# A planner that lets parts of a TensorE block finish on their own, a floor folded into a factor, and a new table of moved turns

## The chip, the cores and the metric

The kernel runs on one core of a Trainium2 chip. The metric is the device time of one execution in microseconds (us); three executions of the kernel before took 788.7, 790.91 and 790.98 us, median 790.91. Engines are named as the profile names them: PE (TensorE; PEld are its weight loads), DVE (VectorE), ACT (ScalarE), POOL (GpSimd) and SP (SyncE, which here only issues DMAs).

## What is computed

Block-sparse attention over 4 batches, 8 heads, 768 positions and head size 64, followed by a feed-forward layer over the 3072 tokens:

```python
scores = scale * np.matmul(q, k.transpose(0, 1, 3, 2))
scores = np.where(mask, scores, -1000000000.0)
attn = np.exp(scores - np.max(scores, axis=-1, keepdims=True))
attn = attn / (np.sum(attn, axis=-1, keepdims=True) + 1e-09)
x = np.matmul(attn, v)            # (4, 8, 768, 64) -> (3072, 512)
h = x @ w_in                      # (512, 2048)
out = np.maximum(0.01 * h, h) @ w_out
```

A query block of 32 positions sees its neighbours, the first and the last block, and three drawn blocks; the first and the last query block see all keys. The weights come in as 64-bit floats and are decoded on the chip.

## The kernel before

**The work.** Every wide product is made of 16-bit halves: an operand is scaled by a power of two, rounded to a high half, and the rest is kept as a low half, so that a product is two or three 16-bit matmuls. The scale comes from a *sum*: ACT squares the tile and adds along the row, `scale_sum` (L699) adds over the 128 rows by a 32-bit matmul with a matrix of ones into a corner of a PSUM bank, and `scale_of` (L706) takes half the exponent on DVE, multiplies by 2^50 and takes the reciprocal. So that a sum of nothing gives no infinity, `scale_sum` first multiplies the ones with a tiny constant tile, `floor` (L696), into the same place. There are 52 such sums: 24 for halves of q, 16 for k, 8 for the weights, 4 for v.

**The units.** Queries go in 12 tiles T of 64 positions for each batch, four tiles make an *item* (12 items), and in a tile the 8 heads make 4 units, two of which make a pair. A unit is: two score products on PE (`s`, keys and queries in both halves, in quarters of the array), mask, scale and minimum on DVE (`p`, `mx`), exponent on ACT (`p`, `sum`), normalising, splitting in halves on ACT and DVE (`pp`), transposing (`pt`: by PE in the first 16 units, later by a DMA that SP issues), and the product with gathered values on PE (`av`, in halves of the array). After the last pair of a tile, ACT, DVE, ACT and POOL make the halves of `x` from `av` (`avt`, `xf`, `x`). When an item's four tiles are done, its feed-forward layer can run: blocks of 12 matmuls `h<-x,W`, then `ht` (ACT, DVE), `g` (DVE or ACT, POOL), then blocks of 6 matmuls `o<-W,g`. Items 0 and 1 run it quarter by quarter, as the weights become ready.

**The weights.** Each quarter of `w_in` and `w_out` is loaded, decoded on ACT and DVE, summed (`sq` products and a sum on PE, `ssw`) and split. For four of the eight quarters the low half is made on PE: `h<-W,dg` (32-bit, 128x512), `h<-W,eye`, into one bank that ACT has to empty (`W<-h`) before the next such block may write it. There are 16 of these *low-half blocks*.

**What sets the order.** The function records all work as tasks (class `Task`, L149; `Plan.task` and `Plan.add`). A PE `block()` joins several matmuls into one task, up to the scores of two units and the `av` of an earlier pair. `Plan.trial` (L328) then plays the tasks on a model of the engines, with costs written down in `COST`, and takes the ready task with the smallest number on each engine; the order that comes out is issued as it is, and each engine runs its own queue in that order. Before a PE task may start in the model, a margin is added when what released it was a DMA (`margin`, 900 ns) or when it is a sum (`margin_sum`, 1500 ns). `SHIFTS` (L168) is a table of (engine, time, length, amount): `Plan.order` (L484) adds the amount to the numbers of the tasks that a first trial started in that time, and runs the trial again. In the kernel before, a joined task releases everything that depends on it when all of it has ended, and its mode of the array is that of its last member:

```python
g.busy += busy + (COST["change"].get((g.kind, kind), 0) if g.run[1:] else 0)
g.late = late
g.kind = kind
```

Of the kernel before, what the change touches and what calls it, by code (L numbers as in the profile page):

```python
# [27 lines left out]
TINY = 2.0 ** -60  # L28
# [120 lines left out]
class Task:  # L149
    __slots__ = ("eng", "run", "busy", "late", "reads", "writes", "prio", "kind", "loads", "need", "then", "n", "gate",  # L150
                 "port")
# [5 lines left out]
    "margin": 900.0,  # L157
    "margin_sum": 1500.0,
# [10 lines left out]
    ("SP", 4453, 107, -1500), ("ACT", 155, 28, 250), ("ACT", 1623, 42, 250), ("all", 2175, 27, 250),  # L169
    ("ACT", 1595, 75, -250), ("PE", 3567, 8, 250), ("all", 6881, 11, -60), ("POOL", 2481, 37, -1500),  # L170
    ("DVE", 2721, 75, -250), ("PE", 6073, 3, -900), ("all", 4828, 11, 500), ("DVE", 3064, 28, 500),
    ("all", 5445, 45, 500), ("all", 3572, 11, 500), ("PE", 6937, 2, 500), ("all", 5557, 144, -500),
    ("SP", 2109, 9, 1500), ("all", 3954, 10, -120), ("PE", 7061, 46, 900), ("PE", 4358, 7, 500),
    ("SP", 1544, 125, 250), ("DVE", 3641, 14, -500), ("PE", 3570, 156, 120), ("DVE", 439, 83, 250),
    ("all", 1197, 83, 60), ("all", 3834, 40, -1500), ("PE", 2617, 26, -500), ("all", 4058, 9, -500),
    ("DVE", 4951, 4, -1500), ("all", 7040, 6, 1500), ("SP", 1817, 33, -250), ("all", 1599, 39, 120),
    ("ACT", 2034, 160, -500), ("all", 3979, 53, -500), ("ACT", 823, 3, 1500), ("PE", 2781, 20, -1500),
    ("DVE", 1339, 35, 1500), ("PE", 4476, 23, -500), ("PE", 4234, 54, -30), ("PE", 6696, 16, -500),
    ("all", 6350, 25, -60), ("DVE", 3344, 34, -900), ("ACT", 654, 7, 500), ("SP", 4785, 91, -500),
    ("DVE", 857, 84, 500), ("POOL", 3003, 70, 250), ("all", 3974, 83, 30), ("PE", 3328, 4, -250),  # L180
    ("DVE", 4105, 2, -1500), ("all", 1984, 11, -1500), ("PE", 3910, 108, 30), ("ACT", 4072, 54, 500),
    ("PE", 1273, 116, 900), ("PE", 1646, 2, -1500), ("PE", 5096, 36, 120), ("all", 7064, 64, 900),
    ("DVE", 1867, 192, 1500), ("POOL", 669, 93, -900), ("SP", 5579, 138, 900), ("ACT", 711, 129, -500),
    ("PE", 4092, 28, -30), ("PE", 2891, 45, 900), ("ACT", 1809, 27, -1500), ("PE", 2615, 16, 500),
    ("PE", 242, 38, 1500), ("all", 5757, 48, 250), ("DVE", 681, 191, 120), ("all", 1863, 25, -250),
    ("PE", 3995, 27, 500), ("SP", 739, 12, -500), ("DVE", 2593, 12, -1500), ("POOL", 143, 58, -1500),
    ("all", 4808, 128, -250), ("all", 5582, 105, 900), ("all", 7636, 41, 250), ("ACT", 2745, 174, 250),
# [3 lines left out]
    ("DVE", 6056, 7, -1500), ("DVE", 2679, 12, -500), ("POOL", 683, 26, 1500), ("all", 5932, 143, 120),  # L191
    ("PE", 5689, 13, 500), ("all", 6366, 5, 250), ("DVE", 1298, 4, 60), ("ACT", 2130, 10, 1500),
    ("DVE", 5753, 47, -900), ("PE", 4075, 46, -60), ("all", 5372, 4, -250), ("PE", 5734, 101, -120),
    ("all", 3970, 3, 120), ("PE", 6430, 172, -250), ("all", 131, 68, 900), ("all", 65, 92, 120),
    ("ACT", 4121, 11, -250), ("PE", 5573, 139, -120), ("PE", 2951, 76, -1500), ("DVE", 5810, 37, 900),
    ("all", 6716, 21, -1500), ("SP", 1552, 11, -1500), ("SP", 136, 8, -500), ("all", 4371, 54, 30),
    ("all", 4733, 84, -120), ("all", 4547, 19, -250), ("PE", 4602, 93, 60), ("all", 1807, 15, -60),
    ("PE", 4207, 100, 120), ("PE", 5966, 6, 250), ("DVE", 5925, 3, 500), ("all", 6695, 132, -60),
    ("DVE", 4349, 101, -1500), ("all", 4763, 97, 60), ("ACT", 2129, 13, 500), ("ACT", 4420, 147, -60),
    ("all", 4756, 16, 250), ("all", 3010, 5, 1500), ("all", 5803, 120, 30), ("all", 2525, 13, -900),  # L200
    ("PE", 2438, 62, -60), ("SP", 2869, 195, 1500), ("POOL", 4611, 7, 1500), ("POOL", 2710, 114, 500),
    ("PE", 4304, 5, 250), ("DVE", 2744, 140, -900), ("PE", 5737, 55, 60), ("DVE", 376, 5, -500),
    ("POOL", 3144, 20, 900), ("all", 5714, 4, 500), ("PE", 7203, 8, 1500), ("all", 134, 126, 1500),
    ("DVE", 2375, 119, -1500), ("DVE", 2552, 6, 900), ("DVE", 2551, 8, -1500), ("PE", 5631, 87, 250),
    ("SP", 2697, 169, 500), ("ACT", 2503, 45, -1500), ("all", 1624, 29, -250), ("SP", 1855, 73, 900),
    ("POOL", 724, 24, -60), ("DVE", 3566, 39, 60), ("DVE", 2426, 132, -900), ("SP", 2127, 28, 500),
# [3 lines left out]
    ("all", 2131, 13, -500), ("DVE", 5346, 193, 250), ("all", 1563, 83, -250), ("ACT", 1620, 84, -30),  # L210
    ("all", 2583, 13, 250), ("DVE", 4829, 140, 900), ("PE", 2578, 30, -250), ("DVE", 735, 14, -900),
    ("all", 767, 51, -250), ("all", 5404, 5, 1500), ("all", 0, 121, -1500), ("PE", 3062, 14, 500),
    ("all", 758, 37, -250), ("all", 5575, 15, -1500), ("DVE", 778, 4, 500), ("all", 3842, 25, 900),
    ("all", 3298, 16, 900), ("all", 1710, 3, -1500), ("DVE", 2941, 124, 500), ("DVE", 2096, 9, 1500),
    ("DVE", 898, 54, 1500), ("SP", 106, 7, 900), ("SP", 5620, 11, 900), ("all", 4754, 152, 60),
    ("PE", 4115, 68, -900), ("PE", 5237, 5, -500), ("all", 2823, 6, 1500), ("all", 7288, 42, 120),
    ("all", 105, 8, -1500), ("all", 3761, 45, -30), ("PE", 5743, 31, 250), ("ACT", 2345, 6, 1500),
    ("all", 4021, 87, 500), ("all", 4084, 29, -500), ("ACT", 1983, 162, -900), ("ACT", 3007, 29, 1500),
    ("PE", 4982, 46, -500), ("all", 129, 44, -250), ("PE", 4110, 92, -500), ("all", 5578, 7, 1500),
    ("SP", 79, 4, 1500), ("all", 3562, 12, 250), ("all", 2681, 4, 500), ("PE", 3379, 195, -60), ("POOL", 837, 5, 60),  # L220
    ("DVE", 4095, 107, -30), ("all", 2632, 7, 250), ("SP", 749, 13, 900), ("SP", 4851, 192, 900),
    ("PE", 4409, 15, -250), ("DVE", 2501, 150, 250), ("PE", 3618, 10, -900), ("DVE", 4553, 8, -1500),
    ("PE", 5456, 27, -250), ("all", 4402, 3, 250), ("all", 180, 9, -500), ("POOL", 718, 6, 900), ("PE", 5497, 9, 500),
    ("PE", 3378, 27, 500), ("all", 835, 6, -250), ("ACT", 4560, 49, -900), ("ACT", 5706, 92, 1500),
    ("DVE", 4151, 81, 120), ("all", 0, 101, -900), ("all", 57, 4, 30), ("PE", 5545, 31, 250), ("PE", 5488, 185, -30),
    ("POOL", 3172, 124, -500), ("DVE", 5716, 40, -500), ("all", 3342, 17, -30),
# [27 lines left out]
class Plan:  # L254
# [10 lines left out]
    def task(self, eng, run, busy, late, reads, writes, kind="", loads=(), port=False):  # L265
        if self.group is not None and eng == self.group.eng:
            g = self.group
            g.run.append(run)
            g.busy += busy + (COST["change"].get((g.kind, kind), 0) if g.run[1:] else 0)
            g.late = late  # L270
            g.reads |= reads
            g.writes |= writes
            g.kind = kind
            g.loads += loads
            return
        t = Task()
        t.eng, t.run, t.busy, t.late, t.kind, t.loads, t.port = eng, [run], busy, late, kind, list(loads), port
        t.reads, t.writes = reads, writes
        self.add(t)

    def add(self, t):
        t.prio, t.n, t.then, t.gate = self.prio, len(self.tasks), [], self.gate
        self.prio += 1.0
        need = set()
        for c in t.reads:
            need.update(self.wrote.get(c, ()))
# [41 lines left out]
    def trial(self, prio, stay):  # L328
# [102 lines left out]
        while events:  # L431
# [24 lines left out]
            elif what == "landed":  # L456
# [3 lines left out]
                if not need[i]:  # L460
                    finish(t, i)
# [1444 lines left out]
```

## Time and profile before

| | us |
|---|---|
| median of three executions | 790.91 |
| lowest and highest | 788.7, 790.98 |
| the profiled execution | 783.51 |
| its span, first to last instruction | 781.5 |
| PE busy | 724.3 (93%) |
| DVE busy | 546.0 (70%) |
| ACT busy | 471.0 (60%) |
| POOL busy | 364.1 (47%) |

The page gives one profiled execution. A row of a group or of the timeline names the engine, the operation, `out<-in` by the program's tile names, the shape, the count, and for a group the busy time and the mean of one; in square brackets stands how long the engine had been idle before, and who ended that. PE's ends are modelled; its starts are not. All work recorded by the planner stands under one line, L531 in the kernel before and L502 in the changed one, so groups are told apart by their tiles.

### The profile page before, as it was taken

Reading aid. Unit: us, or ns where it says so; the run is one execution under the profiler, and the core shown is the slowest. Engines: PE = TensorE matmul, PEld = TensorE weight load, DVE = VectorE, ACT = ScalarE, POOL = GpSimd, SP = SyncE. Lnnn points to the kernel's source line nnn. Section 1 sums busy time; section 2 is a strip of 40 time slices with the busy share of each in tenths; the row PEclk is TensorE's granted clock in tenths of the full one; section 3 lists DMA queues with packets and bytes.
Section 4 is the critical chain, followed back from the end, with each engine's and each line's share of the span. In section 5 each row is a group of like instructions: output and inputs, shape, how many; then the busy total and the mean of one; then the engine's idle time right before and its main releaser. Section 6 shows DMA issues by size and latency. Waiting matters only on the chain. (4 is left out here: it accounts for less than half of the span.)

```text
span 781.5 us, 21520 instructions
## 1 busy us (share of the span) xinstructions
PE 724.3 (93%) x8036; PEld 486.8 (62%) x8036; DVE 546.0 (70%) x1545; ACT 471.0 (60%) x1111; POOL 364.1 (47%) x626
## 2 busy tenths in 40 slices
PE   5575799898999999999999999999999999999997
PEld 5353545466566666666666757666766767666664
DVE  4888679798966787679666677778766766763131
ACT  7789578785874667667466566666565555452111
POOL 4407343444735375566434465555335655442131
PEclk9677599999999999999999999999999999999999
DMA  9629768996879699997996898979675764644100
GB/s 198 246 79 274 215 203 174 231 200 139 195 165 208 97 190 190 217 190 148 200 189 129 135 198 170 205 139 205 147 150 99 147 158 89 136 99 60 34 1 28
DMA packets 261940, 122.64 MB, mean 157 GB/s; under 512 B 230220, under 2 KB 242636, under 8 KB 261836
## 3 DMA queue, kind: packets, MB, share of 16 engines
q1 hardware_dynamic: 254796, 98.20, 62.4%
q0 software_dynamic: 7040, 23.07, 11.7%
q8 instruction: 63, 1.03, 0.6%
q14 instruction: 41, 0.34, 0.2%
HBM read 65.65 MB, written 12.58 MB: 100 GB/s over the span
## 5 line engine op out<-in xcount | busy, mean ns | idle before, releaser
L531 PE MATMUL h<-x,W 128*128 128x256 f16 x2304 | 271.7, 274 | 6.8 <-ACT x L531 3.0
L531 PEld LDWEIGHTS <-W 128*128 128x128 f16 (+1 forms) x2480 | 239.0, 100 | 58.2 <-issue 17.4
L531 PE MATMUL o<-W,g 128*128 128x512 f16 x1152 | 265.6, 379 | 0.3 <-DVE W L531 0.2
L531 POOL TENSOR_TENSOR g<-ht,g 128x512 f16<-128x512 f32 x96 | 116.2, 1211 | 221.8 <-DVE g L531 116.5
L531 PEld LDWEIGHTS <-g 128*128 128x128 f16 x1152 | 109.6, 98 | 122.5 <-issue 6.8
L531 DVE SCALAR_TENSOR_TENSOR pp<-p,r,pp 128x256 f16<-128x256 f32 (+1 forms) x208 | 123.2, 622 | 24.9 <-ACT pp L531 24.4
L531 ACT ACTIVATE p<-p,mx 128x256 f32<-128x256 f32 (+1 forms) x208 | 107.2, 517 | 39.8 <-DVE mx L531 39.1
L1258 POOL DMA_INDIRECT vg<-scr,vrow x88 | 91.1, 1036 | 75.9 <-PE av L531 60.5
L531 ACT ACTIVATE ht<-h,gs 128x512 f32<-128x512 f32 x80 | 54.8, 685 | 116.3 <-PE h L531 73.7
L531 DVE SCALAR_TENSOR_TENSOR ht<-h,gd,ht 128x512 f32<-128x512 f32 x80 | 59.9, 749 | 92.4 <-ACT ht L531 91.9
L531 ACT ACTIVATE pp<-p,r 128x256 f16<-128x256 f32 (+1 forms) x208 | 98.2, 515 | 36.6 <-issue 14.3
L1225 POOL COPY kg<-kt 128x128 int32 x264 | 82.2, 348 | 63.3 <-PE s L531 60.7
L531 DVE CUSTOM_DVE_ANT_0 p<-s,em,nsc 128x256 f32<-128x256 f32 x176 | 80.5, 477 | 12.9 <-PE s L531 12.2
L531 PE MATMUL av<-pt,vg 128*64 128x64 f16 (+1 forms) x2112 | 54.9, 208 | 3.3 <-ACT pp L531 1.9
L531 PEld LDWEIGHTS <-vg 128*64 128x64 f16 x2112 | 46.0, 114 | 14.5 <-issue 13.6
L531 PE MATMUL s<-kg,qs 128*32 128x256 f16 x704 | 47.2, 281 | 7.7 <-DVE r L531 3.0
L531 PEld LDWEIGHTS <-qs 128*32 128x32 f16 (+1 forms) x768 | 25.5, 96 | 38.7 <-issue 31.7
L531 DVE COPY kg<-kt 128x512 f16<-128x512 f16 x96 | 46.4, 506 | 0.8 <-PE s L531 0.8
L531 PE MATMUL s<-kg,qxs 128*32 128x256 f16 x704 | 46.4, 276 | 0.4 <-DMA qxs<-qs 0.4
L531 DVE CAST g<-ht 128x512 f16<-128x512 f32 x80 | 35.4, 443 | 14.5 <-PE o L531 11.4
L531 POOL TENSOR_TENSOR x<-xf,x 128x256 f16<-128x256 f32 x48 | 36.2, 755 | 20.0 <-ACT x L531 19.6
L531 ACT ACTIVATION_READ_ACCUMULATOR p<-p,mx 128x1 f32 x208 | 39.4, 189 | 0.0
(132 smaller groups left out, 783.7 us busy)
## 6 DMA issues: line engine op xcount, KB each, us to landing
v<-in_v_dram SPq DMA_DIRECT2D x32, 192.0 KB
qxs<-qs SPq DMA_DIRECT2D x48, 128.0 KB
scr<-v SPq DMA_DIRECT2D x16, 384.0 KB
vg<-scr SPq DMA_DIRECT2D x44, 128.0 KB
rq<-in_q_dram SPq DMA_DIRECT2D x20, 256.0 KB
W<-in_moe_w_in_dram SPq DMA_DIRECT2D x5, 1024.0 KB
out_dram<-ob SPq DMA_DIRECT2D x20, 256.0 KB
rk<-in_k_dram SPq DMA_DIRECT2D x24, 192.0 KB
```

The costliest lines, as they stand in the source:

```text
L531: self.plan.task(self.eng, lambda: f(*a, **k), busy, late, reads, writes, kind, loads, port)
L1225: tc.nc.gpsimd.tensor_copy(out=kg.ap.bitcast(I32)[:, :, slot * BLOCK // 2:(slot + 1) * BLOCK // 2], in_=kt.ap.bitcast(I32)[:, :, bass.ds(o ...
L1258: tc.nc.gpsimd.indirect_dma_start(into.ap, None, scr[b].ap, bass.IndirectOffsetOnAxis(ap=at.ap, axis=0))
```

## The change

1. A joined PE task is kept as parts, one for each set of places that its members write. A part has its own end, and what depends on it is released then. A task also keeps the mode that it enters with and the one that it leaves with.
2. The margins go from 900 to 300 ns and from 1500 to 500 ns.
3. `SHIFTS` is another table, of 131 rows where there were 234.
4. The product with `floor` is left out of all 52 sums; in its place the DVE instruction that multiplies by 2^50 takes a maximum with `FLOOR` as its second operation.
5. `Plan.latest`, which nothing called, is gone.

```diff
-TINY = 2.0 ** -60
+FLOOR = 2.0 ** -44
...
+    def more(self, run, busy, late, reads, writes, kind, loads):
+        self.busy += COST["change"].get((self.kind, kind), 0) if self.run else 0
+        self.enter, self.kind = self.enter if self.run else kind, kind
+        part = self.parts.setdefault(frozenset(writes), Part())
+        part.begin, part.late = self.busy, late
+        part.reads |= reads
+        part.writes |= writes
+        self.run.append(run)
+        self.busy += busy
+        self.loads += loads
...
-    "margin": 900.0,
-    "margin_sum": 1500.0,
+    "margin": 300.0,
+    "margin_sum": 500.0,
...
-    ("SP", 4453, 107, -1500), ("ACT", 155, 28, 250), ("ACT", 1623, 42, 250), ("all", 2175, 27, 250),
+    ("all", 4829, 75, 250), ("PE", 5937, 140, 1500), ("SP", 1424, 95, 1500), ("all", 3892, 29, -900),
...
-        for i in need:
-            self.tasks[i].then.append(t.n)
+        for i, n in need:
+            self.tasks[i].then[n].append(t.n)
...
-        def finish(t, i):
-            end[i] = t
+        def finish(t, i, part):
+            end[i] = max(end[i], t)
             landed_now[0] = bool(tasks[i].loads)
-            less(t, tasks[i].then)
+            less(t, tasks[i].then[part])
...
-                best = min(ready[e], key=lambda j: prio[j] + (stay if tasks[j].kind != mode[0] else 0.0))
+                best = min(ready[e], key=lambda j: prio[j] + (stay if tasks[j].enter != mode[0] else 0.0))
...
-                at(at0 + late, "done", best)
+                for i, part in enumerate(k.parts):
+                    at(at0 + part.begin * (busy / k.busy) + part.late, "done", (best, i))
...
-    floor = cst.tile([P, 4], F32, name="floor")
-    nc.vector.memset(floor, TINY / P)
-
     def scale_sum(ss, n, name):
         pb = slot_of("sum")
-        with plan.block():
-            nc.tensor.matmul(pb[:, :n], ones, floor[:, :n], start=True, stop=False)
-            nc.tensor.matmul(pb[:, :n], ones, ss, start=False, stop=True)
+        nc.tensor.matmul(pb[:, :n], ones, ss, start=True, stop=True)
         return pb
...
-        nc.vector.tensor_scalar(out=inv[:, :m], in0=ex[:, :m].bitcast(F32), scalar1=2.0 ** 50, scalar2=None, op0=ALU.mult)
+        nc.vector.tensor_scalar(
+            out=inv[:, :m], in0=ex[:, :m].bitcast(F32), scalar1=2.0 ** 50, scalar2=FLOOR, op0=ALU.mult, op1=ALU.max)
```

What the new order looks like, at three places. First PE at the last low-half blocks of the third quarter of `w_out` (`dg` is the diagonal of the scale, `h2` the one bank of these blocks, `g1` the activations of item 0). Before:

```order
L531 MATMUL h2_69<-W_85,dg_191 128x512
L531 LDWEIGHTS eye16_77
L531 MATMUL h2_69<-W_85,eye16_77 128x512
L531 MATMUL h2_69<-W_85,dg_191 128x512
L531 LDWEIGHTS eye16_77
L531 MATMUL h2_69<-W_85,eye16_77 128x512
L531 LDWEIGHTS g1_210
L531 MATMUL o0_65<-W_85,g1_210 128x512
```

and now:

```order
L502 MATMUL h2_69<-W_84,dg_190 128x512
L502 LDWEIGHTS eye16_76
L502 MATMUL h2_69<-W_84,eye16_76 128x512
L502 LDWEIGHTS g1_209
L502 MATMUL o0_65<-W_84,g1_209 128x512
...
L502 MATMUL h2_69<-W_84,dg_190 128x512
L502 LDWEIGHTS eye16_76
L502 MATMUL h2_69<-W_84,eye16_76 128x512
L502 LDWEIGHTS g1_209
L502 MATMUL o1_66<-W_84,g1_209 128x512
```

Four of these blocks stood in a row; now a block of `o`, six matmuls, stands between two of them.

Second PE where item 1 passes from attention to its feed-forward layer (`av0` is its last product with values, `x1` its input, `x0` that of item 0). Before:

```order
L531 MATMUL av0_70<-pt5_155,vg0_89 64x128
L531 LDWEIGHTS qs0_103
L531 MATMUL s0_63<-kg0_87,qs0_103 32x256
...
L531 MATMUL s0_63<-kg0_87,qxs0_104 32x256
L531 LDWEIGHTS W_85
L531 MATMUL h0_67<-x1_211,W_85 128x256
```

and now:

```order
L502 MATMUL av0_70<-pt5_154,vg0_88 64x128
L502 LDWEIGHTS W_84
L502 MATMUL h2_69<-x0_182,W_84 128x256
...
L502 MATMUL s0_63<-kg0_86,qs0_102 32x256
...
L502 MATMUL s1_64<-kg0_86,qs0_102 32x256
...
L502 MATMUL h2_69<-x0_182,W_84 128x256
...
L502 MATMUL h0_67<-x1_210,W_84 128x256
```

Between the last `av` of item 1 and its first `h` there was one score block; now there are three score blocks and two `h` blocks of item 0.

Third ACT around the last `x` of item 0, with which its feed-forward layer can start (`p`, `pp` with 128x256 are softmax of tile 4, `wi1_s` is the scale of the second quarter of `w_in`). Before:

```order
L531 ACTIVATE pt1_140<-o1_66 128x512
L531 ACTIVATE avt_176<-av0_70 128x256
L531 ACTIVATE qa_99<-rq1_105,sc_s3_127 128x8x64
L531 ACTIVATE W_85<-kt0_86 128x1024
L531 ACTIVATE x0_183<-xf_178 128x4x64
L531 ACTIVATE W_85<-W_85,wi1_s_189 128x2x512
L531 ACTIVATE dg_191<-eye_76,neg0_190 128x128
L531 ACTIVATE W_85<-W_85,wi1_s_189 128x2x512
```

and now:

```order
L502 ACTIVATE p0_114,sum0_117<-p0_114,mx4_155 128x256
L502 ACTIVATE p1_115,sum0_117<-p1_115,mx5_157 128x256
L502 ACTIVATE pp0_136<-p0_114,r0_135 128x256
L502 ACTIVATE pt1_139<-o1_66 128x512
L502 ACTIVATE W_84<-kt0_85 128x1024
L502 ACTIVATE pp1_137<-p1_115,r0_135 128x256
L502 ACTIVATE avt_175<-av0_70 128x256
L502 ACTIVATE p2_128,sum1_143<-p2_128,mx0_116 128x256
L502 ACTIVATE W_84<-W_84,wi1_s_188 128x2x512
L502 ACTIVATE dg_190<-eye_75,neg0_189 128x128
L502 ACTIVATE W_84<-W_84,wi1_s_188 128x2x512
L502 ACTIVATE x0_182<-xf_177 128x4x64
```

Five softmax instructions of tile 4, which belongs to item 1, and three of the weight split now stand ahead of the last `x` of item 0.

## Rows read from the trace of the kernel before

**Rows 1.** The page's first part: busy time and share of the span by engine.

```profile
PE 724.3 (93%) x8036; PEld 486.8 (62%) x8036; DVE 546.0 (70%) x1545; ACT 471.0 (60%) x1111; POOL 364.1 (47%) x626
```

**Rows 2.** Windows by stage: us; busy PE, PEld, DVE, ACT, POOL; granted clock, DMA share, GB/s.

```profile
0.00:20.00 20.00, 10.65 (x68) 10.06 (x68) 9.09 (x34) 14.05 (x24) 8.60 (x36) 1.00 1.01 198
20.00:86.00 66.00, 41.91 (x530) 29.22 (x530) 56.93 (x154) 54.84 (x114) 28.63 (x60) 0.68 0.67 217
86.00:200.00 114.00, 101.36 (x1055) 64.76 (x1056) 93.20 (x244) 83.01 (x180) 48.77 (x89) 0.94 0.84 185
200.00:777.00 577.00, 570.37 (x6387) 382.79 (x6385) 386.82 (x1115) 318.41 (x794) 278.12 (x443) 1.00 0.73 144
```

**Rows 3.** Windows of the tile floor: us; busy PE, PEld, DVE; granted clock, DMA.

```profile
0.00:86.00 86.00, 5.10 (x22) 4.61 (x22) 0.06 (x1) 0.76 0.75 212
86.00:200.00 114.00, 4.23 (x24) 3.81 (x24) 0.00 (x0) 0.94 0.84 185
200.00:782.00 582.00, 10.87 (x60) 9.18 (x60) 0.00 (x0) 1.00 0.73 143
```

**Rows 4.** Timeline of PE around one sum: start, us, instruction.

```profile
482.58 0.28 PE L531 MATMUL s<-floor,ones 128*128 128x1 f32 x2
482.73 0.36 PE L531 MATMUL s<-ssk,ones 128*128 128x1 f32 x2
```

**Rows 5.** Waits of PE, 86 to 200 us: total, times, longest.

```profile
PE h L531 <- ACT W L531: 3.5, 6, 0.7
PE h L531 <- ACT x L531: 3.0, 2, 1.5
PE h L531 <- POOL x L531: 1.8, 2, 1.1
PE s L531 <- DVE mx L531: 1.5, 3, 0.7
```

**Rows 6.** The longest of PE's waits, 200 to 782 us.

```profile
PE s L531 <- DVE mx L531: 3.3, 7, 1.5
```

**Rows 7.** Timeline of PE at two low-half blocks.

```profile
149.52 1.12 PE L531 MATMUL h<-W,dg 128*128 128x512 f32 x2 [0.69 <-ACT W L531]
...
151.55 1.12 PE L531 MATMUL h<-W,dg 128*128 128x512 f32 x2 [0.69 <-ACT W L531]
```

**Rows 8.** Timeline of PE where item 1 passes to its feed-forward layer.

```profile
176.68 0.67 PE L531 MATMUL av<-pt,vg 128*64 128x64 f16 x24
...
179.42 0.27 PE L531 MATMUL h<-x,W 128*128 128x256 f16 x1 [1.46 <-ACT x L531]
180.46 1.44 PE L531 MATMUL h<-x,W 128*128 128x256 f16 x6 [0.77 <-POOL x L531]
```

**Rows 9.** Chain of waits: two pieces of 24 matmuls, after `av` and after `o`.

```profile
509.59 2.73 PE h L531 x24
...
690.41 2.62 PE h L531 x24
```

**Rows 10.** Timeline of ACT around the last `x` of item 0.

```profile
87.85 0.39 ACT L531 ACTIVATE avt<-av 128x256 f32<-128x256 f32 x1 [2.90 <-PE av L531]
...
89.75 0.42 ACT L531 ACTIVATE x<-xf 128x256 f16<-128x256 f32 x1
90.05 1.15 ACT L531 ACTIVATE W<-W,wi_s 128x1024 f16<-128x1024 f32 x1
91.09 0.40 ACT L531 ACTIVATE dg<-eye,neg 128x128 f32<-128x128 bf16 x1
```

**Rows 11.** The page's costliest groups: one of the softmax instructions on ACT.

```profile
L531 ACT ACTIVATE p<-p,mx 128x256 f32<-128x256 f32 (+1 forms) x208 | 107.2, 517 | 39.8 <-DVE mx L531 39.1
```

**Rows 12.** Timeline of PE and SP: the scores of a pair, its transposes, its `av`.

```profile
265.07 0.28 PE L531 MATMUL s<-kg,qxs 128*32 128x256 f16 x4
...
273.76 2.52 SPq L531 DMA_TRANSPOSE pt<-pp  x2
...
279.25 0.52 PE L531 MATMUL av<-pt,vg 128*64 128x64 f16 x18
```

More of the change, by code (lines that the diff above doesn't have):

```diff
@@ L149, with __init__ @@
 class Task:
-    __slots__ = ("eng", "run", "busy", "late", "reads", "writes", "prio", "kind", "loads", "need", "then", "n", "gate",
-                 "port")
+    __slots__ = ("eng", "run", "busy", "prio", "enter", "kind", "loads", "need", "then", "n", "gate", "port", "parts")
+    def __init__(self, eng, kind="", port=False):
+        self.eng, self.run, self.busy, self.enter, self.kind, self.loads = eng, [], 0.0, kind, kind, []
+        self.port, self.parts = port, {}
+    def more(self, run, busy, late, reads, writes, kind, loads):
[8 more added lines that the diff above has]
+        self.loads += loads
+class Part:
+    __slots__ = ("begin", "late", "reads", "writes")
+    def __init__(self):
+        self.begin, self.late, self.reads, self.writes = 0.0, 0.0, set(), set()
 COST = {
@@ L168 @@
 SHIFTS = (
-    ("SP", 4453, 107, -1500), ("ACT", 155, 28, 250), ("ACT", 1623, 42, 250), ("all", 2175, 27, 250),
[L170 to L183, printed above, removed]
@@ L192 @@
[L192 to L206, printed above, removed]
[3 rows of a table removed]
@@ L210 @@
[L210 to L224, printed above, removed]
@@ L225 @@
-    ("DVE", 4151, 81, 120), ("all", 0, 101, -900), ("all", 57, 4, 30), ("PE", 5545, 31, 250), ("PE", 5488, 185, -30),
-    ("POOL", 3172, 124, -500), ("DVE", 5716, 40, -500), ("all", 3342, 17, -30),
+    ("all", 4829, 75, 250), ("PE", 5937, 140, 1500), ("SP", 1424, 95, 1500), ("all", 3892, 29, -900),
+    ("all", 983, 87, 30), ("all", 1718, 8, -1500), ("all", 5114, 11, 500), ("PE", 6453, 46, 60),
+    ("all", 603, 3, -1500), ("SP", 1661, 96, 900), ("PE", 6944, 9, 500), ("DVE", 2303, 13, 900),
+    ("DVE", 1117, 26, -500), ("DVE", 5097, 122, -1500), ("PE", 3146, 181, -500), ("PE", 5344, 108, 60),
@@ new lines @@
+    ("DVE", 1707, 62, 1500), ("all", 3369, 40, -250), ("all", 2611, 155, 250), ("all", 3339, 55, -500),
[3 rows of a table added]
+    ("all", 5357, 18, 250), ("SP", 3780, 31, 120), ("all", 6743, 17, -900), ("ACT", 1854, 101, 120),
+    ("PE", 5311, 3, -250), ("PE", 5401, 2, -500), ("PE", 3240, 20, 900), ("PE", 5834, 183, -500),
+    ("POOL", 2467, 133, 500), ("all", 2300, 49, 60), ("DVE", 3922, 171, 500), ("all", 3484, 3, -900),
[5 rows of a table added]
+    ("all", 2183, 5, 500), ("all", 1662, 35, -120), ("all", 6264, 28, -1500), ("PE", 3225, 9, -500),
@@ new lines @@
+    ("ACT", 1304, 30, 60), ("PE", 4710, 23, -900), ("all", 3867, 47, 500), ("all", 4281, 5, 250),
+    ("SP", 4488, 19, 500), ("ACT", 4960, 113, 1500), ("ACT", 3944, 195, -500), ("all", 4936, 141, -60),
+    ("all", 4958, 7, -120), ("ACT", 5049, 44, -1500), ("SP", 1759, 22, 900), ("DVE", 1658, 3, -900),
[4 rows of a table added]
+    ("DVE", 1623, 12, 500), ("all", 1562, 22, 250), ("POOL", 5961, 133, 900), ("DVE", 4872, 14, -900),
+    ("all", 5123, 6, 1500), ("all", 5022, 135, 30), ("all", 5421, 12, 500), ("DVE", 2005, 187, 900),
@@ new lines @@
+    ("all", 1466, 18, 900), ("PE", 5389, 9, 250), ("SP", 1608, 40, 900), ("SP", 4853, 168, 900),
+    ("DVE", 1703, 46, 500), ("DVE", 1281, 189, -500), ("DVE", 1716, 8, -1500), ("all", 2184, 6, 1500),
+    ("DVE", 2138, 55, 500), ("PE", 581, 3, 1500), ("PE", 5477, 8, -900), ("SP", 3102, 113, -500),
+    ("POOL", 5199, 5, -1500), ("DVE", 4998, 43, 900), ("PE", 5550, 118, -900), ("ACT", 1543, 46, -500),
+    ("DVE", 5163, 12, 1500), ("PE", 1643, 17, -500), ("ACT", 1643, 56, -1500), ("DVE", 5125, 7, 1500),
@@ L227 @@
+    ("all", 1799, 2, 1500), ("PE", 3406, 3, 500), ("PE", 3405, 62, 60), ("SP", 3088, 99, -120),
+    ("PE", 3360, 158, -250), ("DVE", 3409, 16, -1500), ("ACT", 1647, 53, 1500),
 )
@@ L319, in block @@
             return
-        g = Task()
-        g.eng, g.run, g.busy, g.late, g.kind, g.loads, g.reads, g.writes = eng, [], 0.0, 0.0, "", [], set(), set()
-        g.port = False
-        self.group = g
+        g = self.group = Task(eng)
         yield
@@ L402, in take @@
             k = tasks[best]
-            at0, busy, late = t, k.busy, k.late
+            at0, busy = t, k.busy
             if e == "PE":
-                if k.kind != mode[0]:
-                    at0 += COST["change"].get((mode[0], k.kind), 0)
-                    mode[0] = k.kind
-                b = pace(at0, busy)
-                busy, late = b, late + b - busy
+                at0 += COST["change"].get((mode[0], k.enter), 0)
+                mode[0] = k.kind
+                busy = pace(at0, busy)
             elif k.port:
@@ L465, in trial @@
         return [i for _, i in sorted(begun, key=lambda x: x[0])], start, end
-    def latest(self, start, end):
-        tasks, last = self.tasks, max(end)
-        free = dict.fromkeys(COST["wake"], last)
-        late = [0.0] * len(tasks)
-        behind = {}
-        for k in tasks:
-            if k.gate in self.marks:
-                behind.setdefault(self.marks[k.gate], []).append(k.n)
-        for i in sorted(range(len(tasks)), key=lambda i: (-end[i], -start[i])):
-            k = tasks[i]
-            done = min([last] + [late[j] - COST["wake"][tasks[j].eng] for j in k.then])
-            at = min(done - (end[i] - start[i]), free[k.eng] - k.busy,
-                     *[late[j] - COST["wake"][tasks[j].eng] for j in behind.get(i, ())])
-            late[i] = free[k.eng] = at
-        return late
     def order(self):
```

50 lines of the change are left out of this document (20 added, 30 removed), and 18 rows, old and new, of the table SHIFTS.

## The prediction, made before the result was known

> **What bounds the kernel now.** I read the shares by engine first: PE is busy for 93% of the span, no other engine for more than 70% [rows 1]. An average hides the stages, so I cut the span at 20, 86 and 200 us, where the first inputs have landed, where the first feed-forward block is about to start and where PE has become dense. The reader is to see three regimes [rows 2]. From 20 to 86 us PE is busy 41.9 of 66 us, at a granted clock of 0.68 (a mixture of the two levels, 1.2 and 2.4 GHz), and DVE and ACT are busy 56.9 and 54.8: they make the softmax of item 0 and decode weights, and PE waits for them. From 86 to 200 PE is busy 101.4 of 114, DVE 93.2. From 200 to 777 PE is busy 570.4 of 577 at the full clock: only 6.6 us are idle there. So from 200 us on the time is the work that stands in PE's queue; between 86 and 200 us 12.6 us are idle on PE, and PE's waits tell for whom: ACT emptying the bank of the low-half blocks (3.5 us), ACT and POOL making `x` (3.0 and 1.8), DVE holding the score banks (1.5) [rows 5]. Before 86 us PE has 33 us of idle time, but it counts only as far as the first feed-forward block comes sooner.
>
> I make the sum against the profiled execution, 783.5 us with a span of 781.5; the median of the three executions is 7.4 us above it, and I carry differences over as they are.
>
> **The floor.** 52 products leave PE's queue, each of two recorded passes. Up to 86 us there are 22 records, which lie in time when PE waits for others; I count nothing for them. After it there are 24 + 60 = 84 records, 42 sums [rows 3]. What one costs the queue is read from start to start: `floor` starts at 482.58 and the product behind it at 482.73 [rows 4]. A sum that follows a score block pays about 0.1 more in front of `floor`, but that moves to the product that stays, since it is the change of the array's mode. 42 x 0.15 = **6.3 us off**. Three of them follow a wait that would end no sooner, so the lower bound is 39 x 0.14 = 5.5.
>
> The busy times of these rows give another figure: 4.23 + 10.87 = 15.1 us after 86 us [rows 3], as each row lasts 0.28 [rows 4] though the next begins after 0.15. The Trainium skill (Perfetto Trace Analysis, Tensor Engine Instruction) says that PE's end times are estimated by the profiler and not observed; by that rule the starts are what counts, and the sum goes by them. By the busy times it would be 8.8 us lower.
>
> The floor inside the factor is a second operation of a DVE instruction on one column; it adds no instruction. I cost it at nothing: DVE is idle for 21 us between 86 and 200 us and for 190 afterwards [rows 2].
>
> **Low-half blocks.** 16 blocks share one bank. Where two stand in a row, the second waits 0.69 us for ACT [rows 7]; all such waits come to 3.5 us, six times [rows 5]. In the new order a block of `o` or of `h` stands between them (the first place shown of the change). From start to start two of these blocks need 2.03 us in rows 7; adding up the PE work in the new order, no two of the 16 begin less than 2.0 us apart, where in the old one five did so at 1.2 to 1.6. I take **3.0 off**; the bounds are 0 (ACT is late with the bank all the same) and 3.5.
>
> **From attention to feed-forward.** Item 1's first `h` waited 1.46 and 0.77 us, because only one score block lay between it and the last `av` [rows 8]; item 0's first `h` had the same wait. Together 4.8 us [rows 5]. Now 3.7 us of PE work lies between them for item 1 and 2.2 for item 0, against 0.4 (counted along both orders, an `h` block at 1.31, half of the row in rows 9). The chain behind `av` took 179.42 - 177.35 = 2.1 us to the first half of `x` and 1.0 more to the second [rows 8]. I take **3.5 off**, bounds 0 and 4.8.
>
> **Score blocks.** A pair of score blocks may only start when DVE has read the two banks of the pair before: 1.5 + 3.3 = 4.8 us of waits after 86 us [rows 5, 6]. Pairs that begin within 2 us of PE work of the last one fall from 50 to 26 in the new order. I take **1.5 off**, bounds 0 and 4.8.
>
> **Changes of mode.** Along the orders PE's array changes its mode 283 times before, 288 now. 24 matmuls take 2.73 us behind an `av` and 2.62 behind a block of the same mode [rows 9], so 0.11 each and **0.5 us on**. This speaks against the change, as the planner now counts a block by the mode that it enters with. The Trainium skill (TensorEngine Tiling, Key Properties) says that changing the tiling mode drains the engine; the rows agree with 0.11 us, and by that rule too these 5 are the whole price.
>
> **New waits.** The margins shrink to a third, so that PE's blocks stand closer behind what they need, and PE's queue is in order: a block that waits holds all `h` and `o` behind it. The pairs whose `av` stands less than 17 us of PE work behind their scores rise from 8 to 19 (of 88); in one place the whole path, scores to transposes to `av`, took 279.25 - 265.07 = 14.2 us [rows 12]. I take **2 us on**, four waits of 0.5, which is the mean of the seven in rows 6; bounds 0 and the rival below. On SP no queue moves by more than a dozen places; transposes stay between the same loads.
>
> **The first feed-forward block.** ACT now does five softmax instructions of tile 4 and the split of a weight before the last `x` of item 0 (the third place): 5 x 0.5 [rows 11] + 1.15 + 0.40 + 1.15 [rows 10] is some 5.3 us more ahead of it. Of that 2.9 us fit into the gap before `avt` [rows 10], and 1.4 into an earlier one. So `x` comes about 1 to 2.5 us later. In exchange some 3 us of PE work (score blocks and a low-half block) are done before the first `h` that were done after it. I count **0**, bounds 3 off (all gaps filled, the work ahead pays) and 5.3 on (none filled).
>
> **The sum:** -6.3 - 3.0 - 3.5 - 1.5 + 0.5 + 2.0 + 0 = -11.8. The profiled execution would go from 783.5 to 771.7, and the median from 790.9 to **779 us**. With all the good ends it is -6.3 - 3.5 - 4.8 - 4.8 + 0.5 - 3 = -21.9, 769; with half of the waits left and four more new ones, some -6, 785. This case's own range is 770 to 785.
>
> **The rivals.** A measurement of this kernel can tell about 0.3%, 2.4 us, from no change.
>
> *The waits only change their names.* From 86 to 200 us DVE is busy 82% of the time [rows 2]. If it and not PE's order sets the pace there, a wait for the low-half bank becomes one for a scale or for `mx` a little later, and only the floors count: -6.3 + 0.5 + 2 = -3.8, 787. For it speaks that weights three quarters later need the same DVE work; against it that the low-half blocks wait for ACT, which is busy 73%, and that DVE has 21 us idle. I give it 0.17.
>
> *The first feed-forward block comes late.* If none of ACT's gaps is filled, everything behind it moves by 5.3 us, and the freed waits are swallowed by the later start: -6.3 + 0.5 + 5.3 = -0.5, 790, no change that can be told. For it: ACT's queue is in order, and the weight split waits for a scale that DVE makes just before. 0.11.
>
> *The margins were needed* (slower). They stood for what the model doesn't know of a DMA's landing and of DVE's lateness. If PE now reaches its blocks before the transposed tiles, each such stop is paid in full, since after 200 us PE has no slack. The place is the `av` blocks: 19 pairs with less than 17 us of PE work to cover a path of 14.2 us at its shortest. Should these wait 1 us each, it is 19; with -11.8 (whose 2 for new waits are then in it) the sum is -13.8 + 19 = +5, 796. It decides from 13.8 us of new waits, some 0.7 for each of the 19. For it: in the trace a wait of 1.5 us happened even with the large margins [rows 6]. Against: after 200 us PE lost only 6.6 us in all, and the distances between `h` and `o` are longer now at the short end (at least 5.2 us of PE work, before 3.9). 0.17.
>
> *The change doesn't do what it says.* That the table moves nothing is ruled out by the orders; that the sum's products are hidden is bounded by the 5.5 above, and stands in the second rival.
>
> **How the numbers follow.** The forecast has 0.55, the rivals 0.17, 0.11 and 0.17. Faster by over 0.3%: 0.55 + 0.17 = 0.72; within it 0.11; slower 0.17. The range takes in the forecast's own range, less some of its lowest end, both of the next cases, and the mild half of the slow one: 770 to 794.
>
> **What would show it.** Right: 52 rows `s<-ss..,ones` and none of `floor`; PE's wait of `h` for ACT W under 1 us between 86 and 200 us; none above 1 us for `x` after item 0; PE's idle time after 200 us still at or under 8 us; the first `h` between 88 and 93 us. Wrong: a wait of `av` for a DMA or for `pt` among the first of PE's waits after 200 us would mean the slow rival; the same idle time under other names between 86 and 200 us the first; a first `h` behind 95 us the second.

## The result and the profile after

| | before | changed |
|---|---|---|
| median (4 executions each, same chip) | 790.28 | 768.85 |
| lowest and highest | 788.7, 790.98 | 766.67, 773.73 |
| ratio | | 0.974 (0.969 to 0.979) |
| profiled execution, its span | 783.51, 781.5 | 769.65, 767.7 |
| PE busy | 724.3 | 709.6 |

The change takes 2.6% off, some 20.5 us at 790. The prediction said 11.8 off, 779, with a range from 770 to 794: the direction was right, the size little more than half of what was measured, and 768.85 lies below the range. A second set gave 0.9746 (0.9716 to 0.9776).

The page's first part, after; PE has 104 rows fewer, those of `floor` [rows 1]:

```profile
PE 709.6 (92%) x7932; PEld 473.8 (62%) x7932; DVE 529.3 (69%) x1544; ACT 469.0 (61%) x1111; POOL 375.6 (49%) x626
```

The windows by stage, columns as in [rows 2] (busy PE, PEld, DVE, ACT, POOL; granted clock, DMA share, GB/s):

```profile
20.00:86.00 66.00, 40.58 (x492) 27.04 (x490) 58.63 (x155) 54.98 (x116) 32.24 (x67) 0.84 0.65 199
86.00:200.00 114.00, 108.93 (x1182) 70.44 (x1182) 97.53 (x274) 91.75 (x200) 64.80 (x98) 0.94 0.91 207
```

From 86 to 200 us PE issues 1182 matmuls where it issued 1055, and is idle for 5.1 us where it was for 12.6. DVE, ACT and POOL are busier there too, POOL by 16 us. PE's waits in that stretch (total, times, longest), all that are listed:

```profile
PE h L502 <- ACT dg L502: 2.4, 1, 2.4
PE o L502 <- DVE W L502: 1.1, 1, 1.1
PE s L502 <- DVE mx L502: 0.9, 2, 0.6
PE s L502 <- DVE r L502: 0.7, 1, 0.7
```

Against [rows 5] `h<-ACT W`, `h<-ACT x` and `h<-POOL x`, 8.3 us in all, are gone from the list. The one that leads now was in the list before with

```profile
PE h L531 <- ACT dg L531: 0.4, 1, 0.4
```

From 200 to 782 us a new one leads, where [rows 6] had `s<-DVE mx` with 3.3:

```profile
PE av L502 <- DMA pt<-pp: 5.7, 4, 2.2
PE s L502 <- ACT k L502: 1.3, 1, 1.3
PE s L502 <- DMA qxs<-qs: 1.1, 1, 1.1
PE s L502 <- DVE mx L502: 0.5, 1, 0.5
```

PE's timeline at the first `h` of item 0 (start, us), before:

```profile
90.21 0.37 PE L531 MATMUL h<-x,W 128*128 128x256 f16 x1 [1.52 <-ACT x L531]
91.66 2.50 PE L531 MATMUL h<-x,W 128*128 128x256 f16 x11 [1.07 <-POOL x L531]
```

and now, with the low-half block ahead of it, and below it the first `h` of item 1:

```profile
95.85 2.08 PE L502 MATMUL h<-W,dg 128*128 128x512 f32 x2 [2.35 <-ACT dg L502]
...
98.83 2.53 PE L502 MATMUL h<-x,W 128*128 128x256 f16 x11
...
169.95 2.25 PE L502 MATMUL h<-x,W 128*128 128x256 f16 x19
```

Neither waits for `x`. The first comes 8.6 us later than before, and the 2.6 us that it waited for `x` have in the main changed their name: ACT now makes `dg` and this `x` one behind the other, after the softmax of tile 4, and PE waits 2.35 us for `dg` at the low-half block just ahead. Two more profiles of the changed kernel, `after_again` and `after_pair`, have that wait too (2.35 and 2.36). The first `h` of item 1 came at 179.42 [rows 8] and comes 9.5 us sooner.

### The profile page after: what moved, and what is told of

Read it like the earlier page. It is cut to its first block, busy times and chain, and to the rows that moved or that the text cites. A ratio compares the mean times of both kernels' runs of the same rounds, so it can differ in the third digit from the quotient of the medians.

```text
span 767.7 us, 21318 instructions
## 1 busy us (share of the span) xinstructions
PE 709.6 (92%) x7932; PEld 473.8 (62%) x7932; DVE 529.3 (69%) x1544; ACT 469.0 (61%) x1111; POOL 375.6 (49%) x626
## 5 line engine op out<-in xcount | busy, mean ns | idle before, releaser
L502 PEld LDWEIGHTS <-W 128*128 128x128 f16 (+1 forms) x2480 | 236.1, 100 | 64.1 <-issue 14.7
L502 DVE SCALAR_TENSOR_TENSOR pp<-p,r,pp 128x256 f16<-128x256 f32 (+1 forms) x208 | 114.0, 576 | 35.2 <-ACT pp L502 31.5
L1192 POOL COPY kg<-kt 128x128 int32 x264 | 92.4, 387 | 46.1 <-PE s L502 42.2
L502 PEld LDWEIGHTS <-vg 128*64 128x64 f16 x2112 | 45.8, 114 | 16.3 <-issue 15.6
L502 POOL TENSOR_TENSOR x<-xf,x 128x256 f16<-128x256 f32 x48 | 34.2, 712 | 15.8 <-ACT x L502 15.3
L502 DVE COPY kg<-kt 128x512 f16<-128x512 f16 x96 | 35.2, 379 | 1.4 <-PE s L502 1.3
```

The source lines that it names most:

```text
L502: self.plan.task(self.eng, lambda: f(*a, **k), busy, late, reads, writes, kind, loads, port)
L1192: tc.nc.gpsimd.tensor_copy(out=kg.ap.bitcast(I32)[:, :, slot * BLOCK // 2:(slot + 1) * BLOCK // 2], in_=kt.ap.bitcast(I32)[:, :, bass.ds(o ...
```

## The experiments

Ratios are to the kernel before in the same set of runs. That kernel's median was 784.7 us in the set of `before_again`, `floor_out`, `sum_twice` and `u_parts_300`, which ran on another chip than the other sets of this section, and 789 to 790 in those. The changed kernel was not run in that set, so where its 0.9746 is compared with a ratio from there, medians in us are given too.

### The floor, in both orders

In the kernel before the planner still sees the floor, so its order stays, but PE does not get it:

```diff
         with plan.block():
-            nc.tensor.matmul(pb[:, :n], ones, floor[:, :n], start=True, stop=False)
-            nc.tensor.matmul(pb[:, :n], ones, ss, start=False, stop=True)
+            plan.task("PE", lambda: None, 200.0, 300.0, cells(ones) | cells(floor), cells(pb[:, :n]), "s")
+            nc.tensor.matmul(pb[:, :n], ones, ss, start=True, stop=True)
```

(with the maximum in the factor, as the change has it). In the changed kernel each sum's product is issued twice:

```diff
...
+        run.insert(0, lambda: pe.matmul(to, ones_, ss_, start=True, stop=True))
```

> The kernel before in its own order, with only the 52 products with floor left out of PE's queue and the maximum with FLOOR in the factor. Theory (the starts count): 42 sums behind 86 us x 0.15 = 6.3 us, at most 7.3 with those ahead of it: 783 to 784 us against 790.3. Rival one (the busy times count): 15 us off, 775. Rival two (a sum waits for its squares anyway, the floor was hidden): under 2 us off, 788 or more.

> The changed kernel in its own order, each sum's product done twice into the same place, so that PE does what it did with floor. Theory: 6 to 7 us on, 775 to 776 against 768.9. Rival one (busy times): 12 to 15 on, 781 or more. Rival two (hidden): under 2 on, 771 or less.

> The changed kernel in its own order with each sum's product done twice, once more and with more rounds, as the first comparison (0.985 to 0.992, against 0.972 to 0.978 of the changed kernel) left 6 to 15 us for the 52 products. Theory (0.15 each): 0.982 to 0.984. Rival (about 0.28 each, the busy time): 0.989 or more.

Measured: `floor_out` 0.9941 (0.9913 to 0.9969), which is 4.6 us off (2.4 to 6.8); the medians, 778.42 and 784.68, differ by 6.3. `sum_twice` 0.9885 (0.985 to 0.992), again 0.983 (0.9801 to 0.986), against 0.9746 of the changed kernel: 11 and 6.6 us on. The 11 compares two sets; the median of the first `sum_twice`, 774.2, is 5.4 us above 768.85. The 6.6, from more executions and a set where the kernel before took 790, agrees with the forecast's 6.3, and `floor_out` excludes the 15 us of the busy times. The floor is worth about 5 to 7 us in either order; some 14 of the 20.5 are something else.

### The profile that the sum was made against

> The kernel before, once more, for a second profile. The profiled execution that the sum was made against took 783.5 us, the others 788.7 to 791.0. Theory: the 5 to 7 us between them lie ahead of about 105 us, where PE waits for inputs, DVE and ACT and its clock is reduced, so that from the first o block on (107.9 us in the old trace) to the end this run takes the same 669 us within 2, and PE waits again some 12 us between the first feed-forward block and 200 us. Rival: they are spread over the span, and the part behind the first o block is 673 us or more.

> The kernel before, for a profile from the same set as the next one. Beside the sets so far it took 784.7 or 789 to 790 us, while its two profiles are both of 784. Theory (what the sets differ by lies in the part ahead of the first feed-forward block, where PE's clock changes): if this run takes 788 or more, its first h stands at 95 us or more, and from there to the end it takes the 686.5 us of the older profiles within 1.5. Rival: the first h stands at 90 to 92 us, and what follows is longer.

> The changed kernel, beside it. Theory: its ratio to the kernel before is 0.974 here too, and PE's idle time between 104 and 200 us is 2 to 3 us where the kernel before has 9.

Measured: 784.2, 790.18 and 766.07 us, one execution each. The first took as long as the old profile and so cannot tell the two readings apart (from the first `o` to the end both take 673.6 us; the 669 of the expectation is too low). The last two, from one set, differ by 24. In `before_pair` the first `h` stands at 89.9 us as in the old profile, so the rival holds, and the 6.7 us by which its span is longer are spread: six single stalls between 129 and 542 us, longer than in the old profile by 0.45 to 1.45 us each, make 5.2 of them; `before_again` lacks the same six. One of them, where the old profile shows no wait:

```profile
316.37 0.38 PE L531 MATMUL s<-floor,ones 128*128 128x1 f32 x2 [1.29 <-DVE s L531]
```

The windows from 104 to 200 us, of `before_pair` and of `after_pair`:

```profile
104.00:200.00 96.00, 85.20 (x927) 54.60 (x924) 77.47 (x215) 71.69 (x163) 41.52 (x77) 0.98 0.82 174
```

```profile
104.00:200.00 96.00, 93.04 (x1020) 60.15 (x1018) 83.78 (x233) 78.93 (x172) 58.19 (x87) 1.00 0.87 188
```

PE is idle for 10.8 us there before, 3.0 after. Where the 24 us arise can be estimated, to some 2 us: I add up the start-to-start times of PE's products in these two traces, leaving out those of `floor`, so that both kernels have the same work. The changed kernel then has as much left at about 107 us as the kernel before at 104.3, and at about 188 as the other at 200.3. It is some 3 us behind up to there, gains some 15 in the stretch where weights and attention run together, and some 12 behind it. Of the floors 10 stand in the stretch and 30 behind it, 1.5 and 4.5 us at 0.15 each. In the two profiles shown first the stretch gives 15 too, what is behind it only some 4.

### Waits taken away in PE's queue alone

The prediction priced single waits of PE and said that other PE work put in front of them would take them away. `waits_apart` does just that in the kernel before, after the planner has made its order; nothing on another engine moves (a pair is a PE task and by how many places it goes back; the function that does it is not shown):

```diff
+MOVED = ((645, 2), (643, 1), (594, 1), (1030, 2), (1029, 2))
```

> The kernel before with PE's queue alone changed at three of its waits: a block of o between the second and third and one between the third and fourth low-half block of the last row of four, the squares of a weight between two others (0.69 us of wait each), and the two h blocks of item 0 between the last av of item 1 and its first h (1.46 and 0.77 us of wait). This does two terms of the prediction alone. Theory of the prediction (such a wait is paid in full and goes when other work is put in): 4.3 us off, ratio 0.994 to 0.995, and PE's waits for ACT W, ACT x and POOL x between 86 and 200 us fall from 8.0 to 3.7. Rival (the other engines' queues are as tight as PE's: the wait comes back further on, as it did when five tasks of the changed kernel were moved): ratio 0.998 or more, waits of about the same sum.

Measured: 1.0021 (1.0002 to 1.0039). The rival holds: PE's waits for ACT `W`, ACT `x` and POOL `x` fall to 4.0 us, about as the theory asked, but the whole list between 86 and 200 us adds up to 16.3, where `before_pair` of the same set has 14.1. PE's timeline where the two blocks of `o` now stand between low-half blocks:

```profile
152.80 1.12 PE L557 MATMUL h<-W,dg 128*128 128x512 f32 x2 [0.69 <-ACT W L557]
153.76 0.38 PE L557 MATMUL h<-W,eye 128*128 128x512 f16 x1
155.35 0.60 PE L557 MATMUL o<-W,g 128*128 128x512 f16 x2 [1.21 <-ACT g L557]
156.59 1.04 PE L557 MATMUL o<-W,g 128*128 128x512 f16 x4 [0.64 <-POOL g L557]
157.46 1.02 PE L557 MATMUL h<-W,dg 128*128 128x512 f32 x2
```

and where item 1's last `av` comes before two `h` blocks of item 0 instead of behind them:

```profile
178.72 1.14 PE L557 MATMUL av<-pt,vg 128*64 128x64 f16 x48
182.93 0.29 PE L557 MATMUL s<-kg,qs 128*32 128x256 f16 x4 [3.07 <-DVE mx L557]
...
183.27 5.99 PE L557 MATMUL h<-x,W 128*128 128x256 f16 x38
```

The block behind the `o` no longer waits for the bank [rows 7], but the `o`, pulled forward, waits 1.85 us for `g`. The wait for `x` [rows 8] is gone, but the score block, reached earlier, waits 3.07 for DVE, which makes `mx` when it did. The same was tried in the changed kernel with its largest new waits:

```diff
+MOVED = ((1135, 3), (1290, 2), (1496, 1), (2717, 3), (2852, 1))
```

> The changed kernel with five of PE's tasks moved by one to three places: a sum of squares of k (at 211.7 us, waited 1.3 for ACT), a block of av (at 223.2, 2.2 for its transposes), a score block (at 274.0, 1.05 for the other half of its queries), a block of av (at 479.3, 1.9) and one at 510.5 (1.2) go behind the h, o or score blocks that follow them; the other engines' queues stay as they are. Theory (the new waits are the price of blocks that stand too close behind what they need, and are paid in full): PE's waits behind 200 us fall from 9.9 to 4 or less, and the time by 5 to 6 us, ratio 0.967 to 0.969. Rival (the work waited for comes late by as much for the next in the chain): waits of the same sum with other names, ratio 0.973 or more.

Measured: 0.9745 (0.9718 to 0.9772), the changed kernel's own ratio. The waits of `av` for transposes fall from 5.7 to 0.6 us, but others take their place, and the list behind 200 us adds up to 12 us, not 4:

```profile
PE s L528 <- DVE s L528: 3.9, 3, 1.7
PE s L528 <- DMA kt<-k: 1.9, 2, 1.5
```

Neither set of moves in PE's queue alone gained anything. Both tried a handful of places, and in the first the `o` that was pulled forward had no `g` yet; that no order of PE alone could gain is not shown.

### The planner without its table

All of these have an empty `SHIFTS` and no floor.

> The changed kernel with an empty SHIFTS table: parts, short margins and no floor stay. Theory (the order that the table makes takes away the waits between 86 and 200 us, the planner's new rules alone don't): 778 to 790 us, with 8 us or more of PE's waits between the first feed-forward block and 200 us. Rival (the parts and the margins do it): 772 or less, with under 6 us of waits there.

> The kernel before without its floor and with an empty SHIFTS table: joined ends, margins of 900 and 1500. Against the untabled kernel with parts and short margins (0.992 of the kernel before) it tells what the planner's new rules do by themselves. Theory (the rules take away the waits between the first feed-forward block and 200 us, 12 us in the kernel before): PE waits there 9 us or more, and the time is 6 us or more above the untabled kernel with parts, ratio 1.000 or more. Rival (the rules do nothing that the table didn't do): within 3 us of it, ratio 0.988 to 0.996.

> The kernel before without floor and without a table, with the margins at 300 and 500: joined ends, short margins. Without a table the joined ends with long margins gave 1.007 of the kernel before, the parts with short margins 0.992. Theory (the parts carry most of this 0.015, since a joined task held back scores and products with values until its last matmul): 1.002 or more. Rival (the margins carry it): 0.997 or less.

> The changed kernel without a table, with the margins at 900 and 1500: parts, long margins. Theory (parts): 0.997 or less. Rival (margins): 1.002 or more. Should both this and the kernel with joined ends and short margins lie at either end, the two only help together, or an order's own accidents are larger than either.

| ratio (interval) | margins 900, 1500 | margins 300, 500 |
|---|---|---|
| joined, as before | 1.0066 (1.0041 to 1.0091) | 1.0138 (1.0105 to 1.017) |
| joined, true end | 1.0006 (0.998 to 1.0033) | 0.996 (0.9936 to 0.9984) |
| parts, true ends (the change) | 0.9942 (0.9917 to 0.9968) | 0.9923 (0.9891 to 0.9956) |
| parts, each begin set to nothing | not run | 1.0162 (1.0121 to 1.0202) |

The first and third rows say that the parts carry it: 1.2 and 2.2%. The first two expectations also asked for PE's waits between the first feed-forward block and 200 us. With joined ends and long margins they add up to 9.3 us, as its theory said, with parts and short margins to 3.9, as the rival said (the time, 779.0, is the theory's): these early waits go without any table. Yet the sum of such a list does not tell the time: parts with long margins show 11.6 us there and are only 0.2% slower, 5.8 us in the medians. The shorter margins alone make the joined planner slower. The 0.9923 is of the set at 784.7; its median is 779.0 us, against 784.8 for the 0.9942, 787.2 for the 0.996 and 804.3 for the 1.0162, so that in us the parts are worth more, not less. What the parts change is more than was told ahead of the result: in the kernel before, `g.late` is overwritten by each matmul, and a joined task is "done" at its begin plus the latency of its last matmul alone. By the code's own cost that is 256/2.4 + 2.5 + 180 ns, 0.29 us, after the begin of an `h` block; 24 such matmuls, two blocks, take 2.62 [rows 9], so one ends after 1.31. Where it takes PE at its full clock, the old model let everything behind such a block start about a microsecond too early. The sentence ahead of the prediction that such a task releases what depends on it "when all of it has ended" is not what that code does. `Part.begin` mends it. The second and fourth rows separate the two things, with the first edit below in `u_true_900` and `u_true_300` and the second in `u_parts_early`:

```diff
-            g.late = late
+            g.late = g.busy - busy + late
...
-        part.begin, part.late = self.busy, late
+        part.begin, part.late = 0.0, late
```

> Joined tasks, long margins, no floor, no table (1.007 of the kernel before), with one line changed: what depends on a joined task is released at the begin of its last matmul plus that matmul's latency, as the parts do it, where the kernel before releases it at the begin of the whole task plus that latency, so for an h block of 1.3 us about a microsecond before it has ended. Theory (what the parts bring is that the planner's ends are true; that each part has an end of its own is worth less): 0.999 or less. Rival (it is the own ends): 1.004 or more.

> The same line with the short margins (joined, short margins gave 1.014, parts with short margins 0.992). Theory (true ends): 1.000 or less, since the long margins then have nothing left to stand for. Rival (own ends): 1.006 or more.

> Parts with short margins and no table (0.992), but each part's begin is set to nothing, so that what depends on it is released too early again, as in the kernel before, while each part still has its own end and the task keeps both modes. Theory (true ends): 1.002 or more. Rival (own ends and modes): 0.996 or less.

With short margins the true end alone is worth 1.8%, and parts without it are 2.4% slower than with it. With long margins it is worth 0.6%, and its 1.0006 lies a little above what the theory asked for. The own end of each part adds 0.4 to 0.6%. Each cell is one order, and a planner's order changes everywhere at a small cause, so the single differences are rough; that both columns and both kinds of task point one way is what bears the reading. The long margins did stand for something: for ends that came too early in the model.

### What the table is worth

> The changed kernel once more, beside the others of this set. The kernel before took 790.3 us beside its first runs and 784.7 beside the second set. Theory (what the two differ by is common to all kernels of a set): the ratio stays at 0.974 within 0.005, so 764 where the kernel before takes 785. Rival (the changed kernel is at 769 always): ratio 0.980 or more beside a kernel before of 785.

> The changed kernel with only the 39 rows of its table that take effect before 200 us of the model. The untabled kernel has the early waits gone already but stops before its last feed-forward block (5.4 us of PE's time between 720 and 730 us, and a lower clock after it). Theory (the table's worth lies in the end): the stop stays, 9 us above the changed kernel within 3. Rival (its worth lies early): within 3 us of the changed kernel.

> The changed kernel with only the 92 rows from 200 us of the model on. Theory: the stop before the last feed-forward block is gone, and the time is that of the changed kernel within 3 us. Rival: 6 us or more above it, with waits between 86 and 200 us that the early rows took away.

Measured: the changed kernel 0.9746 (0.9716 to 0.9776), `rows_early` 0.9859 (0.9828 to 0.989), `rows_late` 0.977 (0.9737 to 0.9802); without any row it was 0.9923. The kernel before took 789.2 us in this set, so what the changed kernel does beside one of 785 stays open. The table's worth is 1.8% by the ratios, some 14 us, and 9 us by the medians (779.0 and 769.9). Its 92 late rows give most of that: `rows_late` is 1.9 us above the changed kernel in the median, `rows_early` 8.9. The windows of the untabled kernel near the end show the largest piece:

```profile
720.00:730.00 10.00, 4.62 (x106) 3.31 (x105) 0.85 (x2) 2.29 (x5) 1.34 (x2) 0.84 0.28 80
730.00:740.00 10.00, 10.00 (x72) 7.70 (x70) 2.35 (x4) 1.37 (x2) 1.99 (x2) 0.81 0.00 0
```

The feed-forward work of item 10 has run out there before item 11's attention is done; PE stands still for 5.4 us, and then its granted clock, a mixture of 1.2 and 2.4 GHz, is at 0.81 for another 10. `rows_late` at the same place:

```profile
720.00:730.00 10.00, 10.00 (x115) 7.26 (x114) 1.60 (x3) 2.86 (x5) 1.29 (x3) 1.00 0.15 54
```

All the other untabled kernels and `rows_early` stop there too. The old table had taken this stop away as well (between 690 and 760 us PE is idle for 0.6 us in the kernel before), so it is no gain over the kernel before; against that kernel, it makes every untabled one look slower than it otherwise would. How much of the 14 us besides the floor each of parts, margins and table brings in the changed kernel itself, no run separates.

## Why the prediction was wrong in size

**The floor** (-6.3): right. 4.6 and 6.6 us were measured in the two orders. Counting starts and not busy times was the right choice. The Trainium skill (Perfetto Trace Analysis, Tensor Engine Instruction) says that PE's ends are estimated; both runs agree, as neither comes near the 15.1 us of the busy times.

**Low-half blocks and `x`** (-3.0 and -3.5): this is the step that failed. The waits that I named, 3.5 and 4.8 us, have left the list, though 2.35 of the latter came back at `dg`. The reason was wrong: "In the new order a block of `o` or of `h` stands between them", and so, I took it, PE no longer pays. The same in the old order, at waits of 4.3 us, gave no gain at all. I read each wait as a price that PE pays and PE's order can save; the runs show that at these places the neighbours were as tight, so that a wait taken away on PE alone comes back as one for `g` or `mx` a few microseconds on. Nor was the sum of these waits the measure of what could be gained: the stretch from 104 to 200 us gave some 15 us by the estimate above, where my terms, the floors in it included, came to some 7. Of those 15, 7.8 are idle time of PE in the two windows, 1.5 the floors, and some 2 the clock (0.98 against 1.00 of 96 us); for the rest I have no row. In the changed kernel all queues are in another order, and DVE, ACT and POOL do more in that stretch. That the gain needs all of them to move is argued and not shown: no run moved another engine's queue by itself.

**Score blocks** (-1.5): too small. `s<-DVE mx` falls from 4.8 to 1.4 us behind 86 us.

**Modes of the array** (+0.5): not separated by any run. The trace of the changed kernel has 286 changes of mode, where I counted 288.

**New waits** (+2.0): of the right kind, `av` for transposes, and somewhat larger in the profiles shown first (9.9 us of listed waits behind 200 us, 6.4 before), not larger in the pair (7.9 against 9.6 of `before_pair`). By my own sign, `av` for a DMA first among the waits behind 200 us, the slow rival should have won; it led the list with only 5.7 us.

**The first feed-forward block** (0, at worst 5.3 on): wrong, it came 8.6 us later, behind the 95 us that I had named for the rival. It did not carry the end with it, since PE had other blocks to do meanwhile: by the estimate above the changed kernel is 3 us behind at 104 us in the pair, 5 in the profiles shown first, near the 5.3 of my worst case.

**The margins were needed** (the slow rival): its ground was sound for the old model, where short margins cost 0.7%. I did not see that the change mends what they stood for, because I took the old release for the end of the task and did not read `g.late = late` against the length of a block.

**The base**: the sum was made against 783.5 us and carried over to 790.9. That was fair, since the difference between two such profiles is spread over the span; but it hides that the pair of one set differs by 24 us, and the two profiles shown first by 13.9.

## What to carry to other kernels

A wait in a profile names only the last link of a chain; before counting it as a gain, ask what the engine would meet next, and take a wait at its full price only if the queues behind it have slack. When a scheduler's model is changed, compare each of its release times with a row of the trace: ends that were a microsecond early cost 0.6 to 2.4% here, while the table was worth 1 to 2%. And an order that is tuned by a table should be compared with the table emptied, on both sides, or the table's worth is taken for the rule's.

## What I had not expected of the hardware

In three executions of the very same program the granted clock from 20 to 86 us was 0.68, 0.82 and 0.55, and the first `h` stood at 90.21, 91.67 and 89.92 us: the lowest clock did not make it later. PE was busy for 41.91, 43.03 and 45.42 of the 66 us, so that over 20 us were idle in each. The windows of the second and the third, with their first `h` (the first execution's stand in [rows 2] and in the section on the result):

```profile
20.00:86.00 66.00, 43.03 (x517) 29.77 (x518) 57.23 (x157) 54.29 (x115) 29.09 (x62) 0.82 0.66 209
...
91.67 0.37 PE L531 MATMUL h<-x,W 128*128 128x256 f16 x1 [1.52 <-ACT x L531]
```

```profile
20.00:86.00 66.00, 45.42 (x524) 31.15 (x525) 56.82 (x154) 54.50 (x114) 29.16 (x62) 0.55 0.67 213
...
89.92 0.37 PE L531 MATMUL h<-x,W 128*128 128x256 f16 x1 [1.92 <-ACT x L531]
```

And the same program's medians lay at 784.7 us in one set and at 789 to 790 in five others. Between a profile of that set, `before_again`, and `before_pair` the difference is in the six stalls told of above, behind DVE in four of them and POOL in two. What makes these engines late there in one run and not in the next, and whether it goes with the chip, was not found.
